# A fused FFT and two-layer kernel on one Trainium2 core: the beginning rearranged, with the first stage's stores ahead of the second weight chunk

## The chip, the cores and the metric

The kernel runs on 1 core of one Trainium2 chip (trn2). The metric is the time of one execution in device microseconds; below, "us" is microseconds. The core has a matrix engine (TensorE, PE in the profile, with its weight loads as PEld), a vector engine (VectorE, DVE), an activation engine (ScalarE, ACT), a general engine (GpSimd, POOL), and a queue engine (SyncE, SP) that issues most of the DMA transfers.

## The reference, cut to what matters

```
X = np.fft.fft(x, axis=1)            # x: (2, 3008, 256)
X = np.fft.fft(X, axis=2)
x = X.real.astype(np.float32).reshape(6016, 256)
h = x @ w_in                         # (256, 2048)
g = np.where(h > 0, h, np.exp(np.minimum(h, 0)) - 1)
x = g @ w_out                        # (2048, 256)
h = x @ w2_in
g = np.maximum(h, 0) + alpha * np.minimum(h, 0)
return g @ w2_out
```

The weights arrive as 64-bit floats, x as 32-bit floats.

## The kernel before

**The transform.** 3008 is 47 times 64, so the transform along the sequence is done in two stages. Stage A (`stage_a`) multiplies a chunk `xc` of x by the 47-point matrix `f47` on TensorE; ScalarE copies the result to `uc`; `store_u` writes it to memory (`ud`) with two axes exchanged, and `load_v` reads it back as `vt`, transposed. Batch 0 has four such chunks c = 0 to 3, each done in two halves i = 0, 1. Stage B (`stage_b`) multiplies `vt` by the 64-point matrix `r64`, in two halves q = 0, 1; ScalarE and VectorE split each result into a high and a low part (`zt`). The 256-point transform along the other axis isn't done on the data: it is multiplied into the first weights (`w_fold`: `c256` times a chunk of `w_in` gives `wi`, also as a high and a low part). `w_fold` also sends a row by memory to `an_sb`, which VectorE needs in the ticks. `delta_0` and `spread_0` make a correction row `zb`.

**The weights.** `w_in` and `w_out` are loaded (`ld`) in four chunks of 1 MB each. Before a chunk can be used, its 64-bit numbers are made 32-bit ones, half a chunk at a time: `conv_y` is one ScalarE instruction (L308), `conv_s` three VectorE ones (L325, L327, L329); `conv_h` does all four. For `w_out`, `w_split` then makes the high part on ScalarE (L380) and the low one on GpSimd (L381).

**The ticks.** Layer 1 is 96 ticks, one for each pair of a block of columns and a tile f of 128 hidden units. Tick t does, on TensorE, `gemm1` (L422, two banks of three multiplications) and at its end `gemm2` (L438, twelve) of tick t-3 (tick 0's stands at the end of tick 2). VectorE makes from the two banks `pt` (L555) and two tiles `ht` (L556, L557); ScalarE makes the exponential (L574, L576); VectorE combines (`combine`, L527), ScalarE splits off the high part (L534), GpSimd the low part (`lo`, L540). Tick 5 begins with stage B of the second block, and a small ScalarE copy `dt` (L218) of its correction. The second layer follows in 48 pairs.

**What sets the order.** Each engine works through its own list in the order in which the code is written. The list `START` is the order of the beginning; the tables `CONV1`, `FOLD` and others hang further steps into ticks, at their beginning (`pre`), middle (`mid`) or end (`end`). Fold c = 0 serves hidden tiles 0 to 3, fold 1 tiles 4 to 7 (first used in tick 4). PSUM has two banks `mmt` and two banks `eet` for everything but `gemm2`; `mmtile` hands them out in turn.

SyncE issues a transfer only when its wait has ended, and what stands behind it in the list waits too. Before the change the four stores of stage A of batch 0 are issued by ScalarE.

Of the kernel before, what the change touches and what calls it, by code (L numbers as in the profile page):

```python
# [28 lines left out]


START = [
# [3 lines left out]
    ('conv', 'i', 1, 0), ('conv', 'i', 1, 1), ('fold', 0), ('an', 0), ('fold', 1), ('delta',),  # L35
    ('conv', 'o', 0, 0),
    ('alpha',), ('u', 1), ('load', 'o', 1, 1), ('b',), ('conv', 'o', 0, 1), ('split', 'o', 0, 0), ('v', 1, 0, 32), ('load', 'x', 1, 0), ('u', 2),
    ('load', 'i', 1, 2), ('load', 'x', 1, 1), ('load', 'o', 1, 2), ('load', 'x', 1, 2), ('load', 'i', 1, 3), ('load', 'o', 1, 3),
    ('an', 1),
]  # L40


# [3 lines left out]


CONV1 = [
    (('o', 1, 0), None, (None, None, 1)),
    (('o', 1, 1), (3, 3, 5), (4, 4, 6)),  # L50
    (('i', 1, 2), (8, 8), (9, 9)),
    (('o', 1, 2), (13, 13, 15), (14, 14, 15)),
# [5 lines left out]
    (0, (7, 'pre'), (8, 'pre')), (1, (9, 'pre'), (11, 'pre')), (2, (12, 'pre'), (14, 'pre')), (3, (16, 'pre'), (17, 'pre')),  # L58
]
LOAD_X = {3: 9}  # L60
FOLD = {2: (11, 'pre', 0), 3: (18, 'pre', 0)}
LOAD_V = {(0, 2): 12, (1, 0): 24, (1, 1): 24, (1, 2): 24}
STAGE_B = {(0, 1): 5, (0, 2): 22, (1, 2): 32, (1, 0): 36, (1, 1): 40}
LOAD_ZB = {1: 6, 2: 29, 3: 45, 4: 61, 5: 77}
# [37 lines left out]
def tile_fft_moe_elu_moe_prelu(  # L102
# [72 lines left out]
    uc = {}  # L175

    def stage_a(b, c, i):

        if i == 0:
            uc[b, c] = big.tile([96, 8, 256], F32, tag="big", name="uc")  # L180
        for r0 in (4 * i, 4 * i + 2):
            p = mmtile()
            mm(out=p[0:96], lhsT=f47_sb, rhs=xc[b, c][0:96, r0:r0 + 2, :].rearrange("p r j -> p (r j)"),
               start=True, stop=True)
            act(out=uc[b, c][:, r0:r0 + 2, :].rearrange("p r j -> p (r j)"), in_=p[0:96], func=ACTF.Copy)
        if i == 1 and b == 1:
            for g in range(3):
                store_u(b, c, g)
        if i == 1 and b == 0:
            store_u(b, c, 0, nc.scalar)  # L190

    def store_u(b, c, g, eng=nc.sync):
        eng.dma_start(out=ud[b][g][c * 8:(c + 1) * 8].rearrange("n m j -> m n j"),
                      in_=uc[b, c][g * 32:(g + 1) * 32])


    vt = {}
# [58 lines left out]
    def stage_b(b, g):  # L256
        v = vt.pop((b, g))
        bl = BL[b, g]
        z = big.tile([128, 2, 2, 512], F32R, tag="big", name="zt")
        for q in range(2):  # L260
            p = mmtile()
            for k in range(4 * q, 4 * q + 4):
                o = p.rearrange("p (e k n) -> p e k n", e=2, k=4)[:, :, k % 4, :]
                mm(out=o, lhsT=v[:, k, 0:128], rhs=r64_sb[:, 0:128], start=True, stop=False)
                mm(out=o, lhsT=v[:, k, 128:256], rhs=r64_sb[:, 128:256], start=False, stop=True)
            pv = p.rearrange("p (e m) -> p e m", e=2)
            own = BLOCKS[bl][2] - (MOVED if bl == LONG else 0)
# [12 lines left out]
        zt[bl] = z  # L280
# [4 lines left out]

    def ld(kind, layer, c, eng):

        home, tag = (big, "big") if (kind, layer, c) in wd else (wp, f"w{kind}{c}")
        if kind == "i":
            src = (w_in, w2_in)[layer - 1][:, c * 512:(c + 1) * 512].bitcast(I32).rearrange("(k p) f -> p k f", p=128)  # L290
            t = home.tile([128, 2, 1024], I32, tag=tag, name="w64")
        else:
            src = (w_out, w2_out)[layer - 1][c * 512:(c + 1) * 512, :].bitcast(I32).rearrange("(k p) d -> p k d", p=128)
            t = home.tile([128, 4, 512], I32, tag=tag, name="w64")
        eng.dma_start(out=t, in_=src)
        raw[kind, layer, c] = t
        w32[kind, layer, c] = None
# [38 lines left out]
    def w_fold(c):  # L336

        t = w32.pop(("i", 1, c)).rearrange("p (k f) -> p k f", k=2)
        w = wp.tile([128, 2, 2, 512], F32R, tag=f"wi{c}", name=f"wi{c}")
        for e in (1, 0):  # L340
            p = mmtile()
            for k in range(2):
                mm(out=p, lhsT=c256_sb[:, k, e * 128:(e + 1) * 128], rhs=t[:, k, :], start=(k == 0), stop=(k == 1))
            if e == 1:
                at_ = wk.tile([1, 512], F32, tag="s", name="at", bufs=4)
                act(out=at_, in_=p[0:1, :], func=ACTF.Copy)
                nc.scalar.dma_start(out=ad[:, c * 512:(c + 1) * 512], in_=at_)
# [195 lines left out]
    def tick(t, pre, mid, end):  # L543
# [3 lines left out]
        if cur:  # L547
# [171 lines left out]
    with tc.manual_schedule():  # L719
# [192 lines left out]
```

## Time and profile before

| | |
|---|---|
| median of 3 runs | 976.53 us (976.29 to 977.09) |
| profiled execution, its own time | 976.22 us |
| its span | 974.3 us |
| TensorE busy | 952.8 us, 98% of the span |
| VectorE busy | 724.2 us, 74% |
| ScalarE busy | 653.4 us, 67% |
| GpSimd busy | 623.7 us, 64% |

The span runs from the first to the last instruction that the profile shows; the execution's own time is 1.9 us longer. A busy share is a mean over the whole span; the beginning, with which the change deals, is a small part of it and looks different.

### The profile page before, as it was taken

Reading aid. Unit: us, or ns where it says so; the run is one execution under the profiler, and the core shown is the slowest. Engines: PE = TensorE matmul, PEld = TensorE weight load, DVE = VectorE, ACT = ScalarE, POOL = GpSimd, SP = SyncE. Lnnn points to the kernel's source line nnn. Section 1 sums busy time; section 2 is a strip of 40 time slices with the busy share of each in tenths; the row PEclk is TensorE's granted clock in tenths of the full one; section 3 lists DMA queues with packets and bytes.
Section 4 is the critical chain, followed back from the end, with each engine's and each line's share of the span. In section 5 each row is a group of like instructions: output and inputs, shape, how many; then the busy total and the mean of one; then the engine's idle time right before and its main releaser. Section 6 shows DMA issues by size and latency. Waiting matters only on the chain.

```text
span 974.3 us, 12247 instructions
## 1 busy us (share of the span) xinstructions
PE 952.8 (98%) x4206; PEld 768.2 (79%) x4206; DVE 724.2 (74%) x1045; ACT 653.4 (67%) x925; POOL 623.7 (64%) x497
## 2 busy tenths in 40 slices
PE   9899999999999999999999999999999999999998
PEld 3576767789888877788878878889988887887886
DVE  2797989989999999887767766566756656566564
ACT  5577776676788878898766655555566565565553
POOL 1365667765777869887788755656656574664543
PEclk9999999999999999999999999999999999999999
DMA  8963322202212411121140020020010002001001
GB/s 322 332 207 83 90 77 87 98 1 87 60 58 80 167 44 33 44 86 44 44 152 1 1 81 1 1 87 1 1 45 38 1 1 87 1 2 43 1 1 44
DMA packets 27014, 64.11 MB, mean 66 GB/s; under 512 B 3076, under 2 KB 11524, under 8 KB 24776
## 3 DMA queue, kind: packets, MB, share of 16 engines
q1 hardware_dynamic: 25536, 62.09, 19.0%
q10 hardware_dynamic: 1160, 1.07, 0.4%
q8 instruction: 33, 0.54, 0.2%
q0 software_dynamic: 256, 0.17, 0.1%
q14 instruction: 29, 0.24, 0.1%
HBM read 41.53 MB, written 21.79 MB: 65 GB/s over the span
## 4 chain that ended last, share of the span: by engine, by line
PE 76%; DVE 14%; issue 4%; ACT 3%; DMA 3%; SPq 0%; POOL 0%; DVEq 0%; ACTq 0%
PE acc L438 43%; PE eet L611 13%; PE mmt L611 9%; PE mmt L422 7%; DVE ht L557 2%; DVE et L524 2%; DVE pt L555 2%; PE eet L422 2%; DVE et L527 1%; DMA w<-w_in 1%; DVE w L329 1%; DVE sg L327 1%; DVE sg L325 1%; DMA w<-w_out 1%; ACT hi L629 1%
## 5 line engine op out<-in xcount | busy, mean ns | idle before, releaser
L438 PE MATMUL acc<-hi,wo 128*128 128x512 f32 (+1 forms) x1536 | 469.5, 387 | 5.4 <-ACT hi L534 2.4
L635 POOL TENSOR_TENSOR lo<-et,hi 128x512 fp32r<-128x512 f32 (+1 forms) x190 | 237.2, 1280 | 187.0 <-ACT hi L629 187.0
L438 PEld LDWEIGHTS acc<-hi,wo 128*128 128x128 f32 x1536 | 288.7, 188 | 61.8 <-ACT hi L534 2.8
L540 POOL TENSOR_TENSOR lo<-et,hi 128x512 fp32r<-128x512 f32 (+1 forms) x192 | 267.3, 1415 | 102.5 <-ACT hi L534 50.4
L438 PE MATMUL acc<-lo,wo 128*128 128x512 f32 (+1 forms) x768 | 297.6, 388 | 2.8 <-POOL lo L540 2.6
L629 ACT ACTIVATE hi<-et 128x1024 fp32r<-128x1024 f32 (+1 forms) x96 | 99.5, 1043 | 115.9 <-PE acc L438 60.3
L438 PEld LDWEIGHTS acc<-lo,wo 128*128 128x128 f32 x768 | 144.8, 189 | 33.9 <-POOL lo L540 6.2
L574 ACT ACTIVATE et<-ht 128x1024 f32<-128x1024 f32 (+2 forms) x97 | 100.3, 1034 | 81.9 <-DVE ht L557 76.3
L656 DVE TENSOR_TENSOR v<-mmt,p 128x512 f32<-128x512 f32 (+1 forms) x48 | 32.7, 682 | 144.1 <-ACT p L652 143.9
L422 PE MATMUL mmt<-zt,wi 128*128 128x512 f32 (+1 forms) x462 | 122.8, 397 | 2.9 <-DVE ht L557 1.0
L422 PEld LDWEIGHTS mmt<-zt,wi 128*128 128x128 f32 x462 | 85.7, 188 | 27.0 <-DVE ht L557 4.4
L534 ACT ACTIVATE hi<-et 128x1024 fp32r<-128x1024 f32 (+2 forms) x97 | 99.2, 1023 | 3.9 <-DVE et L527 2.6
L677 ACT ACTIVATE et<-mmt 128x512 f32<-128x512 f32 (+1 forms) x96 | 55.9, 589 | 31.2 <-PE mmt L611 16.3
L527 DVE SCALAR_TENSOR_TENSOR et<-et,ht 128x1024 f32<-128x1024 f32 (+2 forms) x44 | 69.2, 1574 | 1.8 <-POOL lo L540 1.1
L555 DVE SCALAR_TENSOR_TENSOR pt<-zb,an_sb,mmt 128x512 f32<-128x512 f32 (+1 forms) x77 | 56.3, 732 | 14.9 <-PE mmt L422 14.6
L524 DVE SCALAR_TENSOR_TENSOR et<-eet,ht 128x512 f32<-128x512 f32 (+1 forms) x106 | 67.2, 676 | 0.0
L680 DVE SCALAR_TENSOR_TENSOR et<-et,oma_sb,eet 128x512 f32<-128x512 f32 (+1 forms) x96 | 66.3, 732 | 0.0
L680 DVE SCALAR_TENSOR_TENSOR et<-et,oma_sb,mmt 128x512 f32<-128x512 f32 (+1 forms) x96 | 66.1, 730 | 0.0
L581 ACT ACTIVATE eet<-et 128x512 f32<-128x512 f32 (+1 forms) x106 | 58.9, 588 | 3.7 <-DVE et L524 2.1
L611 PE MATMUL mmt<-xo,wi 128*128 128x512 f32 (+1 forms) x216 | 60.2, 387 | 1.0 <-ACT p L652 1.0
L611 PE MATMUL eet<-xo,wi 128*128 128x512 f32 (+1 forms) x216 | 60.2, 387 | 0.0
L611 PE MATMUL eet<-xo,sx 128*128 128x512 f32 (+1 forms) x216 | 59.7, 385 | 0.0
(120 smaller groups left out, 1287.5 us busy)
## 6 DMA issues: line engine op xcount, KB each, us to landing
w<-w_in SPq DMA_DIRECT2D x8, 1024.0 KB, 5.9
w<-w_out SPq DMA_DIRECT2D x8, 1024.0 KB, 7.7
vt<-ud SPq DMA_DIRECT2D x6, 1024.0 KB, 4.8
ud<-uc SPq DMA_DIRECT2D x20, 256.0 KB, 4.2
xd<-xs SPq DMA_DIRECT2D x10, 512.0 KB, 3.1
xs<-xd SPq DMA_DIRECT2D x5, 1024.0 KB, 8.4
out_t<-ot SPq DMA_DIRECT2D x16, 256.0 KB, 2.2
xc<-x SPq DMA_DIRECT2D x5, 768.0 KB, 7.9
```

Of the source, the lines that this page charges most:

```text
L422: mm(out=p[:, 0:n], lhsT=lhsT, rhs=rhs, start=(i == 0), stop=(i == len(ops) - 1))
L438: mm(out=accs[L, bl][d][t][:, 0:n], lhsT=w[:, a, o, d * 128:(d + 1) * 128], rhs=(hi, lo)[b][:, t, 0:n], start=(f == first and i == 0), sto ...
L524: stt(out=s["e"][:, i, :], in0=s["x"][i], scalar=-1.0, in1=s["h"][:, i, :], op0=ALU.add, op1=ALU.max)
L527: stt(out=s["e"][:, i], in0=s["e"][:, i], scalar=-1.0, in1=s["h"][:, i], op0=ALU.add, op1=ALU.max)
L534: act(out=s["hi"][:, i, 0:s["n"]], in_=s["e"][:, i], func=ACTF.Copy)
L540: nc.gpsimd.tensor_tensor(out=s["lo"][:, i, 0:n], in0=s["e"][:, i, :], in1=s["hi"][:, i, 0:n].bitcast(F32), op=ALU.subtract)
L555: stt(out=pt[:, 0:n], in0=zb[bl][:, 0:n], scalar=an_sb[:, f:f + 1], in1=p[0], op0=ALU.mult, op1=ALU.add)
L574: act(out=s["e"][:, i], in_=s["h"][:, i], func=ACTF.Relu, scale=-1.0)
L611: mm(out=bank[:, 0:n], lhsT=w[:, a], rhs=x2[b][:, 0:n], start=(first and m == 0), stop=(last and m == 2), skip_group_check=True)
L629: act(out=s["hi"][f][:, :, 0:n], in_=s["g"][f], func=ACTF.Copy)
L635: eng.tensor_tensor(out=s["lo"][f][:, t, 0:n], in0=s["g"][f][:, t], in1=s["hi"][f][:, t, 0:n].bitcast(F32), op=ALU.subtract)
L680: stt(out=o, in0=o, scalar=oma_sb[:, 2 * j + f:2 * j + f + 1], in1=h, op0=ALU.mult, op1=ALU.add)
```

## The change

It rewrites the order of the beginning.

- The four stores of stage A of batch 0 go from ScalarE's queue to SyncE's, where they stand ahead of the load of the second chunk of `w_in` (before, that load was issued at the start). The store of the last chunk is cut in two, one for each half i.
- The transposed read `vt` is cut in two: its rows 0 to 24 of 32, which depend on the first three chunks, and rows 24 to 32.
- Fold 1 leaves the beginning and goes to the start of tick 1, behind `combine(0)`; the conversion of its chunk stands in and behind stage B (one half between its two halves, one half after it).
- The conversion and split of the first `w_out` chunk leave the beginning: half 0 goes to tick 0, half 1 to ticks 2 and 3. The raw chunk is loaded into another buffer (`wo3`).
- `w_fold` works on both banks by turns (first half of the weights for both, then the second half).
- `combine(0)` and the split of tick 0 move from behind tick 1's `pt` and `ht` to the start of tick 1.

```diff
 START = [
-    ('r64',), ('eye',), ('load', 'i', 1, 0), ('c256',), ('load', 'i', 1, 1),
-    ('a', 0, 0), ('a', 0, 1), ('a', 1, 0), ('a', 1, 1), ('a', 2, 0), ('a', 2, 1), ('conv', 'i', 0, 0), ('conv', 'i', 0, 1), ('a', 3, 0),
-    ('a', 3, 1), ('v', 0, 0, 32), ('load', 'o', 1, 0),
-    ('conv', 'i', 1, 0), ('conv', 'i', 1, 1), ('fold', 0), ('an', 0), ('fold', 1), ('delta',),
-    ('conv', 'o', 0, 0),
-    ('alpha',), ('u', 1), ('load', 'o', 1, 1), ('b',), ('conv', 'o', 0, 1), ('split', 'o', 0, 0), ('v', 1, 0, 32), ('load', 'x', 1, 0), ('u', 2),
+    ('r64',), ('eye',), ('load', 'i', 1, 0), ('c256',),
+    ('a', 0, 0), ('a', 0, 1), ('a', 1, 0), ('a', 1, 1), ('a', 2, 0), ('a', 2, 1),
+    ('conv', 'i', 0, 0), ('conv', 'i', 0, 1), ('a', 3, 0), ('a', 3, 1), ('v', 0, 0, 24), ('v', 0, 24, 32),
+    ('load', 'i', 1, 1), ('load', 'o', 1, 0), ('alpha',), ('u', 1), ('load', 'o', 1, 1),
+    ('fold', 0), ('an', 0), ('delta',), ('b',), ('conv', 'i', 1, 1),
+    ('v', 1, 0, 32), ('load', 'x', 1, 0), ('u', 2),
...
 CONV1 = [
-    (('o', 1, 0), None, (None, None, 1)),
+    (('o', 1, 0), (0, 0, 0), (2, 2, 3)),
...
-FOLD = {2: (11, 'pre', 0), 3: (18, 'pre', 0)}
+FOLD = {1: (1, 'pre', 1), 2: (11, 'pre', 0), 3: (18, 'pre', 0)}
...
-        if i == 1 and b == 0:
-            store_u(b, c, 0, nc.scalar)
+        if b == 0 and c == 3:
+            store_u(b, c, 0, rows=(4 * i, 4 * i + 4))
+        elif b == 0 and i == 1:
+            store_u(b, c, 0)
...
             if q == 0 and b == g == 0:
                 spread_0()
+                conv_h("i", 1, 1, 0)
...
-        home, tag = (big, "big") if (kind, layer, c) in wd else (wp, f"w{kind}{c}")
+        home, tag = (big, "big") if (kind, layer, c) in wd else (wp, "wo3" if (kind, layer, c) == ("o", 1, 0) else f"w{kind}{c}")
...
+        banks = {1: mmtile(), 0: mmtile()}
+        for k in range(2):
+            for e in (1, 0):
+                mm(out=banks[e], lhsT=c256_sb[:, k, e * 128:(e + 1) * 128], rhs=t[:, k, :], start=(k == 0), stop=(k == 1))
...
-        if t == 1:
-            combine(0)
-            split_hi(0)
-            split_lo(0)
...
+        at(1, combine, 0)
         for c, (t, where, n) in FOLD.items():
             at(t, w_fold, c, where=where)
             at(t + n, load_an, c, nc.gpsimd, where='end')
+        at(1, split_hi, 0)
+        at(1, split_lo, 0)
```

On SyncE, behind the first loads of x, the list before reads as follows (`w` is a raw weight chunk, `c_sb` the 256-point matrix, `al_sb` a vector that is used much later).

```order
L295 DMA w_129<-w_in 128x2x1024
L745 DMA c_sb<-c 128x2x256
L295 DMA w_132<-w_in 128x2x1024
L203 DMA vt<-ud_81 128x2048
L295 DMA w_203<-w_out 128x4x512
L742 DMA al_sb<-alpha 128x16
L193 DMA ud_82<-uc 32x8x256 x4
L295 DMA w_262<-w_out 128x4x512
```

And now:

```order
L298 DMA w_129<-w_in 128x2x1024
L746 DMA c_sb<-c 128x2x256
L195 DMA ud_81<-uc 32x8x256 x3
L195 DMA ud_81<-uc 32x4x256 x2
L205 DMA vt<-ud_81 96x2048
L205 DMA vt<-ud_81 32x2048
L298 DMA w_203<-w_in 128x2x1024
L298 DMA w_205<-w_out 128x4x512
L743 DMA al_sb<-alpha 128x16
L195 DMA ud_82<-uc 32x8x256 x4
L298 DMA w_212<-w_out 128x4x512
```

The second `w_in` chunk has moved from ahead of the read of `vt` to behind both its parts, and the stores of stage A stand ahead of that read.

On TensorE, from the end of stage A to the correction row (L232), the list before holds two folds (eight multiplications of `c_sb`).

```order
L183 MATMUL mmt<-xc,f_sb 96x512
L343 MATMUL mmt<-w_176,c_sb 128x512 x2
L343 MATMUL eet<-w_176,c_sb 128x512 x2
L343 MATMUL eet<-w_205,c_sb 128x512 x2
L343 MATMUL mmt<-w_205,c_sb 128x512 x2
L232 MATMUL mmt<-r_sb,vt 8x64
```

Now it holds one fold there, and the other stands behind the two banks of tick 0's `gemm1` (L427).

```order
L182 MATMUL mmt<-xc,f_sb 96x512
L346 MATMUL mmt<-w_174,c_sb 128x512
L346 MATMUL eet<-w_174,c_sb 128x512
L346 MATMUL mmt<-w_174,c_sb 128x512
L346 MATMUL eet<-w_174,c_sb 128x512
L234 MATMUL eet<-r_sb,vt 8x64
...
L427 MATMUL eet<-zt,wi_214 128x512 x3
L427 MATMUL mmt<-zt,wi_214 128x512 x3
L346 MATMUL mmt<-w_250,c_sb 128x512
L346 MATMUL eet<-w_250,c_sb 128x512
L346 MATMUL mmt<-w_250,c_sb 128x512
L346 MATMUL eet<-w_250,c_sb 128x512
```

Four multiplications of `c_sb` have left the place between stage A and the correction row.

On VectorE, from tick 0's `pt` to tick 2's, the list before is this.

```order
L555 SCALAR_TENSOR_TENSOR pt<-zb,an_sb,mmt 128x512
L556 TENSOR_TENSOR ht<-pt,eet 128x512
L557 TENSOR_TENSOR ht<-pt,eet 128x512
L555 SCALAR_TENSOR_TENSOR pt<-zb,an_sb,eet 128x512
L556 TENSOR_TENSOR ht<-pt,mmt 128x512
L557 TENSOR_TENSOR ht<-pt,mmt 128x512
L527 SCALAR_TENSOR_TENSOR et<-et,ht 128x512 x2
L555 SCALAR_TENSOR_TENSOR pt<-zb,an_sb,mmt 128x512
```

And now (`w_205` is the first chunk of `w_out`, `wi_321` the result of fold 1):

```order
L560 SCALAR_TENSOR_TENSOR pt<-zb,an_sb,eet 128x512
L561 TENSOR_TENSOR ht<-pt,mmt 128x512
L562 TENSOR_TENSOR ht<-pt,mmt 128x512
L328 TENSOR_SCALAR sg<-w_205 128x512
L330 SCALAR_TENSOR_TENSOR sg<-w_205,sg 128x512
L332 SCALAR_TENSOR_TENSOR w_306<-w_306,sg 128x512
L532 SCALAR_TENSOR_TENSOR et<-et,ht 128x512 x2
L354 TENSOR_TENSOR wi_321<-mmt,wi_321 128x512
L354 TENSOR_TENSOR wi_321<-eet,wi_321 128x512
L560 SCALAR_TENSOR_TENSOR pt<-zb,an_sb,eet 128x512
L561 TENSOR_TENSOR ht<-pt,mmt 128x512
```

Between tick 0's `ht` and tick 1's `pt` three steps of a conversion and two of the fold have come in, and `combine(0)` (`et`) stands ahead of tick 1's `pt`. Half 1 of the same conversion, three more, now stands between tick 2's `combine(1)` and tick 3's `pt`.

## Rows read from the trace of the kernel before

**Rows 1.** The page's first line: the span.
```profile
span 974.3 us, 12247 instructions
```
**Rows 2.** Stretches of the span: length, then each engine's busy time, clock, DMA.
```profile
50.00:60.00 10.00, 8.38 (x53) 6.40 (x52) 9.62 (x12) 5.84 (x7) 5.28 (x4) 1.00 0.85 227
60.00:70.00 10.00, 10.00 (x42) 7.49 (x41) 8.71 (x12) 7.63 (x9) 5.72 (x4) 1.00 0.67 238
```
**Rows 3.** TensorE in time: start, length, instruction, idle before and its releaser.
```profile
42.59 3.16 PE L438 MATMUL acc<-hi,wo 128*128 128x512 f32 x8 [2.37 <-ACT hi L534]
59.65 0.96 PE L422 MATMUL eet<-zt,wi 128*128 128x512 f32 x3 [0.98 <-ACT dt L218]
```
**Rows 4.** TensorE and the queues in time, end of stage A to stage B.
```profile
19.84 0.59 ACT L185 ACTIVATE uc<-mmt 96x512 f32<-96x512 f32 x1
...
22.08 2.74 PE L343 MATMUL eet<-w,c_sb 128*128 128x512 f32 x6
...
23.27 0.34 SPq L203 DMA_DIRECT2D vt<-ud  x1
...
28.16 0.27 PE L232 MATMUL mmt<-r_sb,vt 128*8 128x64 f32 x2 [0.35 <-DMA vt<-ud]
...
30.46 1.12 PE L239 MATMUL eet<-eye 8*128 8x512 f32 x2
...
33.17 0.39 PE L265 MATMUL mmt<-r_sb,vt 128*128 128x128 f32 x2
```
**Rows 5.** DMA issues of short stretches: KB each, us from issue to landing.
```profile
f_sb<-f SPq DMA_DIRECT2D x1, 36.0 KB, 1.7
...
xc<-x SPq DMA_DIRECT2D x1, 256.0 KB, 2.9
...
ud<-uc ACTq DMA_DIRECT2D x1, 256.0 KB, 7.7
...
ud<-uc ACTq DMA_DIRECT2D x1, 256.0 KB, 2.7
...
an_sb<-ad POOLq DMA_DIRECT2D x1, 2.0 KB, 6.1
```
**Rows 6.** VectorE in time, from fold 0 to the first tick.
```profile
24.84 0.69 DVE L349 TENSOR_TENSOR wi<-mmt,wi 128x512 fp32r<-128x512 f32 x1
25.44 0.68 DVE L349 TENSOR_TENSOR wi<-eet,wi 128x512 fp32r<-128x512 f32 x1
...
32.13 0.43 DVE L325 TENSOR_SCALAR sg<-w 128x512 int32<-128x512 int32 x1 [2.37 <-DMA w<-w_out]
...
34.00 0.69 DVE L275 TENSOR_TENSOR zt<-eet,zt 128x512 fp32r<-128x512 f32 x1
...
37.06 0.74 DVE L555 SCALAR_TENSOR_TENSOR pt<-zb,an_sb,mmt 128x512 f32<-128x512 f32 x1
```
**Rows 7.** VectorE in time, ticks 1 to 4.
```profile
45.21 1.23 DVE L527 SCALAR_TENSOR_TENSOR et<-et,ht 128x1024 f32<-128x1024 f32 x1 [0.69 <-ACT et L576]
...
47.92 0.75 DVE L555 SCALAR_TENSOR_TENSOR pt<-zb,an_sb,eet 128x512 f32<-128x512 f32 x1 [1.49 <-PE eet L422]
...
51.11 1.51 DVE L325 TENSOR_SCALAR sg<-w 128x512 int32<-128x512 int32 x1
...
55.13 0.74 DVE L555 SCALAR_TENSOR_TENSOR pt<-zb,an_sb,mmt 128x512 f32<-128x512 f32 x1
```
**Rows 8.** ScalarE in time: fold 1 before.
```profile
26.14 0.59 ACT L346 ACTIVATE at<-eet 1x512 f32<-1x512 f32 x1 [1.54 <-PE eet L343]
...
27.04 0.60 ACT L348 ACTIVATE wi<-eet 128x512 fp32r<-128x512 f32 x1 [0.31 <-ACT at L346]
```
**Rows 9.** GpSimd in time: two pairs of `lo`.
```profile
42.63 2.53 POOL L540 TENSOR_TENSOR lo<-et,hi 128x512 fp32r<-128x512 f32 x2 [3.44 <-ACT hi L534]
...
48.76 3.57 POOL L540 TENSOR_TENSOR lo<-et,hi 128x512 fp32r<-128x512 f32 x2 [1.18 <-ACT hi L534]
```
**Rows 10.** A stretch after the longest idle time of TensorE (columns of rows 2).
```profile
43.30:46.70 3.40, 3.40 (x10) 2.65 (x9) 2.45 (x3) 3.34 (x5) 2.78 (x3) 0.51 1.08 367
```

More of the change, by code (lines that the diff above doesn't have):

```diff
@@ L31 @@
 START = [
[3 rows of a table removed]
-    ('conv', 'i', 1, 0), ('conv', 'i', 1, 1), ('fold', 0), ('an', 0), ('fold', 1), ('delta',),
-    ('conv', 'o', 0, 0),
-    ('alpha',), ('u', 1), ('load', 'o', 1, 1), ('b',), ('conv', 'o', 0, 1), ('split', 'o', 0, 0), ('v', 1, 0, 32), ('load', 'x', 1, 0), ('u', 2),
[6 rows of a table added]
     ('load', 'i', 1, 2), ('load', 'x', 1, 1), ('load', 'o', 1, 2), ('load', 'x', 1, 2), ('load', 'i', 1, 3), ('load', 'o', 1, 3),
-    ('an', 1),
 ]
@@ L188, in stage_a, with store_u @@
                 store_u(b, c, g)
-        if i == 1 and b == 0:
-            store_u(b, c, 0, nc.scalar)
-    def store_u(b, c, g, eng=nc.sync):
-        eng.dma_start(out=ud[b][g][c * 8:(c + 1) * 8].rearrange("n m j -> m n j"),
-                      in_=uc[b, c][g * 32:(g + 1) * 32])
+        if b == 0 and c == 3:
+            store_u(b, c, 0, rows=(4 * i, 4 * i + 4))
+        elif b == 0 and i == 1:
+            store_u(b, c, 0)
+    def store_u(b, c, g, rows=(0, 8)):
+        r0, r1 = rows
+        nc.sync.dma_start(out=ud[b][g][c * 8 + r0:c * 8 + r1].rearrange("n m j -> m n j"),
+                          in_=uc[b, c][g * 32:(g + 1) * 32, r0:r1])
     vt = {}
@@ L339, in w_fold @@
         w = wp.tile([128, 2, 2, 512], F32R, tag=f"wi{c}", name=f"wi{c}")
+        banks = {1: mmtile(), 0: mmtile()}
+        for k in range(2):
+            for e in (1, 0):
+                mm(out=banks[e], lhsT=c256_sb[:, k, e * 128:(e + 1) * 128], rhs=t[:, k, :], start=(k == 0), stop=(k == 1))
         for e in (1, 0):
-            p = mmtile()
-            for k in range(2):
-                mm(out=p, lhsT=c256_sb[:, k, e * 128:(e + 1) * 128], rhs=t[:, k, :], start=(k == 0), stop=(k == 1))
+            p = banks[e]
             if e == 1:
```

## The prediction

> **What bounds the kernel now.** I read the page first, then the stretches of the span, and then the beginning engine by engine in order of time. The span is 974.3 us [rows 1]. From 60 to 70 us TensorE is busy 10.00 of 10 us, from 50 to 60 only 8.38, while VectorE has 9.62 there [rows 2]. So there is a point near 60 us behind which TensorE sets the time, and ahead of which something else does. The last wait before it is the one of the matmul at 59.65 (tick 5's second bank), 0.98 us for ScalarE's `dt` [rows 3]. Behind it the lists of all engines are the same before and after. So the change is worth what it moves this matmul, one for one, and all that follows is about where it goes. The span's own execution took 976.22 us, 0.31 less than the median of the runs; I add the shift to both.
>
> Ahead of that point I follow VectorE by two marks: tick 0's `pt` at 37.06 [rows 6] and tick 4's at 55.13 [rows 7]. From tick 4's `pt` to the matmul at 59.65 (two `ht`, the exponential, `dt`) nothing is edited. From mark to mark it is 18.07 us, in which VectorE waits twice: 0.69 for ScalarE and 1.49 for TensorE [rows 7].
>
> What puts mark one at 37.06? The correction row starts when `vt` has landed, at 28.16, and stage B's first half is done at 30.46 [rows 4]. But its low part comes only at 34.00, since the conversion of the first `w_out` chunk stands ahead of it and that chunk lands at 32.13 [rows 6]. So the beginning waits first for the transposed read, then for a weight chunk that isn't needed yet.
>
> **The read comes sooner.** Stage A ends as now, at 19.84 + 0.59 = 20.43 [rows 4]: its x is loaded ahead of all that moves. Today's last store holds 256 KB and lands in 2.7 us [rows 5]; the read is issued at 23.27, which is 0.14 later [rows 4]. The new last store holds 128 KB. 36 KB took 1.7 [rows 5], so 128 KB lies between 1.7 and 2.7; I take 2.1, on a straight line. The second part of the read is then issued at 20.43 + 2.1 + 0.14 = 22.7. It holds 256 KB, and a load of that size took 2.9 [rows 5]: 25.6. The first part, 768 KB, is issued near 20.9 and has 4.7 us; the whole 1 MB takes 28.16 - 23.27 = 4.9 [rows 4], so it is no later. Correction row at 25.6 (bounds 25.2 to 26.2), 2.5 us sooner.
>
> The other stores cost nothing, though they now stand in one queue behind `w_in` and `c256`: one that was issued beside the loads took 7.7 us already [rows 5], and only the last is waited for. ScalarE's four issues go away in ScalarE's idle time of a stage that TensorE paces.
>
> **From there to tick 0's `pt`.** Stage B's first half takes 30.46 - 28.16 = 2.3 us: 27.9. ScalarE's copy adds 0.6, and VectorE makes the first low part at 28.5. Such an instruction occupies VectorE for 0.60 (24.84 to 25.44), and the three steps of half a conversion for 34.00 - 32.13 = 1.87 [rows 6]. So: first steps of the second `w_in` chunk 29.1 to 31.0; the second half of stage B ends 33.56 - 30.46 = 3.1 us behind the first [rows 4], at 31.0, its copy at 31.6; second low part to 32.2; three more steps to 34.1. Mark one goes from 37.06 to 34.1: **-3.0** (bounds -3.4 and -2.4).
>
> This holds if three transfers come in time. The second `w_in` chunk is issued right behind the read. A chunk in that place (`w_out`) now lands 32.13 - 28.16 = 4.0 us behind the read, which would be 29.6 against 29.1; the 0.6 us for which VectorE waits for stage B covers that. `w_out` follows by at most 4.0, at 33.6, and ScalarE wants it ahead of tick 0's exponential, near 35.5. `an_sb` took 6.1 us from its issue [rows 5], which now comes near 25.5: 31.6, against 34.1. Were one of these covers gone, each microsecond of lateness would count in full, because VectorE and ScalarE work in order.
>
> **Inside the ticks.** Five things change between the marks.
>
> The conversion of the first `w_out` chunk comes in: two halves, 2 x 1.87 = 3.74. Fold 1's two low parts come in: 2 x 0.60 = 1.20. Together **+4.9**. Until now this work stood ahead of mark one, mostly in time in which VectorE waited for `vt` and `w_out` anyway.
>
> The 1.49 us wait for TensorE goes: three conversion steps (1.87) now stand ahead of that very `pt`. The 0.69 wait shrinks to about 0.3: tick 1's exponential takes some 2.2 us after its `ht`, and tick 2's `pt` and two `ht` fill 2.0. Together **-1.9** (bounds -2.2 and -0.7).
>
> A new wait: fold 1's low parts follow ScalarE's high parts. On ScalarE, behind the last conversion step, stand the split of `w_out` (0.5), `at` with its issue (27.04 - 26.14 = 0.90) and a copy of 0.6 [rows 8]: some 2.1 us, while VectorE has two `combine` of 0.6 to do. **+1.0** (bounds 0 and 1.4). Behind it on VectorE stands tick 1's `pt`, and all later ticks wait.
>
> Fold 1's four matmuls, 2.74 / 3 = 0.9 us each [rows 4], go in between two ticks of TensorE. They cost nothing there: TensorE is ahead of VectorE and waits for the banks that VectorE frees. Uncovered they would cost 3.6. That `combine(0)` moves ahead makes ScalarE's and GpSimd's split of tick 0 sooner, but TensorE can use it only behind tick 2's `gemm1`, so it gives nothing. The order within the fold, likewise, moves less than a microsecond on an engine that then waits for the read.
>
> VectorE and GpSimd disturb each other: a step L325 took 1.51 us instead of 0.43 [rows 6, 7], and the pair of `lo` beside it 3.57 instead of 2.53 [rows 9]. The moved steps of half 0 come ahead of the first `lo`, those of half 1 behind tick 0's pair, so I charge 0; the upper bound is two such meetings, +2.2. [...]
>
> **Sum**: -3.0 + 4.9 - 1.9 + 1.0 = +1.0, with the roundings +1.1. The matmul at 59.65 comes near 60.7. The profiled execution would take 977.3 us, the median of the runs 977.6; I predict 977.4, which is 0.1% slower. A measurement of this kernel can tell about 0.2%, or 2 us, from no change: so no change, from what is gained ahead of the ticks and lost in them. For the forecast alone: 976.7 to 978.4.
>
> **Rivals.**
>
> *TensorE's clock falls ahead of stage B (slower).* Fold 0 ends near 19.7 + 3.6 = 23.3, and with fold 1 gone nothing stands between it and the read at 25.6: 2.3 us of idle time. Now the wait there is 0.35 [rows 4]. [...] It decides if the read lands at 25.6 or later; a read at 24.5 would leave half the idle time. [...] Chance 0.25. [...]
>
> *VectorE isn't what binds in the ticks (faster).* Then the 4.9 us hide in waits that I don't see, and the 3.0 ahead of mark one reach the end: 973.5. Against it: 9.62 of 10 us busy [rows 2], and only 2.2 us of waits between the marks. Chance 0.10.
>
> *The read isn't sooner.* If the stores in SyncE's queue wait for the loads ahead of them longer than I think, or two parts cost more than one, `vt` lands at 28.1 as now, and only the loss remains: 1.1 + 2.5, 980.1. Chance 0.05.
>
> *The waits absorb more.* Without the new wait, and with a read at 25.2, the sum lies between -0.6 and +0.2: 976.0 to 976.7. Chance 0.10.
>
> **How the numbers follow.** The forecast has 0.50. Slower by over 0.2% (above 978.5): most of the first rival, the third, and the forecast's edge by meetings with GpSimd, 0.31. Faster by over 0.2% (below 974.6): most of the second, 0.09. Within: 0.60. For 8 in 10 I leave out the second and third rivals and the top of the first: 975.2 to 979.6.
>
> **What would show it.** Right: the correction row starts near 25.6 and tick 0's `pt` near 34; `pt` of tick 4 near 56; VectorE in one piece from 34 to 56, with a wait of about 1 us for ScalarE ahead of fold 1's low parts; the matmul behind `dt` near 60.7. [...] Wrong would be `vt` far from 25.6, a wait of VectorE for `w_in` or `an_sb`, or a tick 4 `pt` at 53 or sooner.

## The result, and the profile after

The changed kernel takes 982.03 us, the median of 6 runs (981.44 to 984.53), against 976.41 for the kernel before: a ratio of 1.0065 (95% interval 1.0051 to 1.0079). It is 5.6 us slower, where 977.4 was predicted and 979.6 was the upper end of the range.

The page's first line, the span:

```profile
span 980.5 us, 12256 instructions
```

TensorE in time, from the last fold to the point behind which it sets the time (start, length, instruction; in brackets the idle time before it and what ended it):

```profile
22.35 1.02 PE L346 MATMUL eet<-w,c_sb 128*128 128x512 f32 x2
28.69 0.37 PE L234 MATMUL eet<-r_sb,vt 128*8 128x64 f32 x2 [5.32 <-DMA vt<-ud]
...
32.92 1.52 PE L241 MATMUL mmt<-eye 8*128 8x512 f32 x2
...
65.60 0.96 PE L427 MATMUL eet<-zt,wi 128*128 128x512 f32 x3 [0.98 <-ACT dt L220]
```

The last row answers to the matmul at 59.65 in [rows 3], and waits for the same `dt` as long as it did: a shift of +5.95. The span grew by 980.5 - 974.3 = 6.2, so nearly all of the loss lies ahead of this point, as the prediction assumed. Within it, the correction row starts at 28.69; 28.16 was its time before [rows 4], 25.6 the forecast. TensorE idles 5.32 us ahead of it.

VectorE in time, the two marks and what lies between them:

```profile
39.55 0.74 DVE L560 SCALAR_TENSOR_TENSOR pt<-zb,an_sb,eet 128x512 f32<-128x512 f32 x1
...
45.60 0.69 DVE L354 TENSOR_TENSOR wi<-mmt,wi 128x512 fp32r<-128x512 f32 x1 [0.86 <-ACT wi L353]
...
51.18 1.23 DVE L532 SCALAR_TENSOR_TENSOR et<-et,ht 128x1024 f32<-128x1024 f32 x1 [0.16 <-ACT et L577]
...
56.23 2.16 DVE L532 SCALAR_TENSOR_TENSOR et<-et,ht 128x1024 f32<-128x1024 f32 x1
...
59.57 1.59 DVE L332 SCALAR_TENSOR_TENSOR w<-w,sg 128x512 int32<-128x512 int32 x1
61.08 0.73 DVE L560 SCALAR_TENSOR_TENSOR pt<-zb,an_sb,mmt 128x512 f32<-128x512 f32 x1
```

Tick 0's `pt` stands at 39.55: 2.49 later than the 37.06 of [rows 6], where the forecast had 3.0 sooner. From mark to mark it is 61.08 - 39.55 = 21.53, against 18.07 before, or +3.46; the forecast was +4.0. So the ticks went as reckoned, and the 5.5 us of error lie ahead of tick 0.

The chain that ended last, from stage A's last store on, shows where they begin:

```profile
20.59 1.95 DMA ud<-uc
...
22.59 5.96 DMA vt<-ud
...
28.69 0.37 PE eet L234 x2
```

The store took 1.95 (forecast 2.1) and the second part of the read was issued at 22.59 (forecast 22.7). But from issue to landing it took 5.96 us, where I had put 2.9. Two stretches of the span, one in the read and one in stage B:

```profile
24.00:27.00 3.00, 0.00 (x0) 0.00 (x0) 1.29 (x2) 0.77 (x2) 0.94 (x1) 0.99 0.94 208
...
26.90:33.70 6.80, 5.01 (x21) 4.32 (x22) 0.73 (x2) 0.60 (x1) 0.78 (x1) 0.50 1.03 359
```

The DMA engines are busy 0.94 of the first stretch and move only 208 GB/s. In the second the granted clock is 0.50 through all of stage B's first half. So two questions: why is the read slow, and what does the low clock cost?

### The profile page after: what moved, and what is told of

Its sections match the earlier page's. It is cut to its first block, busy times and chain, and to the rows that moved or that the text cites. A ratio compares the mean times of both kernels' runs of the same rounds, so it can differ in the third digit from the quotient of the medians.

```text
span 980.5 us, 12256 instructions
## 1 busy us (share of the span) xinstructions
PE 954.7 (97%) x4206; PEld 770.0 (79%) x4206; DVE 724.8 (74%) x1045; ACT 652.8 (67%) x925; POOL 623.0 (64%) x497
## 4 chain that ended last, share of the span: by engine, by line
PE 77%; DVE 12%; ACT 4%; issue 3%; DMA 2%; SPq 0%; POOL 0%; DVEq 0%; ACTq 0%
PE acc L443 44%; PE eet L612 12%; PE mmt L612 9%; PE mmt L427 7%; DVE et L529 2%; DVE ht L562 2%; DVE pt L560 2%; PE eet L427 2%; DMA w<-w_in 1%; DVE w L332 1%; DVE sg L330 1%; ACT et L575 1%; PE eet L182 1%; DVE et L532 1%; ACT hi L630 1%
## 5 line engine op out<-in xcount | busy, mean ns | idle before, releaser
L427 PE MATMUL mmt<-zt,wi 128*128 128x512 f32 (+1 forms) x462 | 122.8, 397 | 4.4 <-DVE wi L354 2.5
L427 PEld LDWEIGHTS mmt<-zt,wi 128*128 128x128 f32 x462 | 85.5, 188 | 28.5 <-DVE ht L562 5.0
```

The lines of the kernel that those rows point to most:

```text
L427: mm(out=p[:, 0:n], lhsT=lhsT, rhs=rhs, start=(i == 0), stop=(i == len(ops) - 1))
```

## The experiments

The marks of every run, from the same rows as above (us; "row" is the correction row's first matmul, "last" the matmul behind `dt`), and the medians. Beside them on the same chip the kernel before took 977.02 (e1 to e4), 976.60 (e5 to e8) and 976.49 (e9, e10); the last column is the distance of each median from that (the changed kernel's from its 976.41). The marks are those of one execution, the profiled one.

| kernel | row | tick 0's pt | tick 4's pt | last | median | over before |
|---|---|---|---|---|---|---|
| before | 28.16 | 37.06 | 55.13 | 59.65 | 976.41 | 0 |
| changed | 28.69 | 39.55 | 61.08 | 65.60 | 982.03 | +5.62 |
| e2_fill | 28.38 | 36.91 | 58.46 | 62.98 | 979.82 | +2.80 |
| e1_one_read | 27.94 | 38.03 | 59.57 | 64.09 | 981.49 | +4.47 |
| e3_one_read_fill | 28.14 | 36.67 | 58.21 | 62.73 | 980.23 | +3.21 |
| e5_cols | 28.24 | 39.01 | 60.54 | 65.06 | 981.49 | +4.89 |
| e6_p64 | 28.67 | 41.50 | 63.05 | 67.57 | 984.97 (one run) | +8.37 |
| e4_conv_only | 28.33 | 35.68 | 54.69 | 59.22 | 977.61 | +0.59 |
| e8_combine | 28.36 | 35.71 | 55.12 | 59.65 | 977.26 | +0.66 |
| e9_fold_only | 28.39 | 37.03 | 59.04 | 63.57 | 982.01 | +5.52 |
| e10_repaired | 28.70 | 35.15 | 56.69 | 61.21 | 978.14 | +1.65 |
| e7_best | 30.51 | 34.92 | 54.33 | 58.85 | 976.10 | -0.50 |

In e7 and e10 the correction row stands behind stage B's first half.

### What the low clock costs: e2_fill

```diff
+    def fill(n):
+        p = pa.tile([128, 512], F32, tag="acc00", name="fill")
+        for i in range(n):
+            mm(out=p, lhsT=c256_sb[:, 0, 0:128], rhs=c256_sb.rearrange("p k f -> p (k f)"), start=(i == 0), stop=(i == n - 1))
...
-    ('fold', 0), ('an', 0), ('delta',), ('b',), ('conv', 'i', 1, 1),
+    ('fold', 0), ('an', 0), ('fill', 6), ('delta',), ('b',), ('conv', 'i', 1, 1),
```

> The changed kernel with six more multiplications of the 256-point matrix by itself on TensorE between fold 0 and the correction row (some 5.2 us of work into a bank that nobody reads), so that TensorE isn't idle while it waits for vt. Theory 1 (the idle time of 5.3 us makes the granted clock fall, and the low clock costs what stage B loses): granted clock 1.0 from 20 to 40 us, stage B's first half 2.3 us instead of 3.9 (from the correction row at 28.7 to the bank's last column), tick 0's pt near 37.7 instead of 39.55, time about 980.1. Theory 2 (the low clock costs nothing, because VectorE and ScalarE set the pace here): pt stays at 39.5, time 982.

TensorE in time and the stretch of stage B in e2_fill:

```profile
23.13 5.31 PE L723 MATMUL fill<-c_sb 128*128 128x512 f32 x12
28.38 0.28 PE L234 MATMUL eet<-r_sb,vt 128*8 128x64 f32 x2
...
30.68 1.12 PE L241 MATMUL mmt<-eye 8*128 8x512 f32 x2
```

```profile
26.90:33.70 6.80, 6.80 (x42) 4.61 (x40) 2.82 (x5) 1.76 (x3) 0.78 (x1) 1.00 1.05 361
```

Work that nobody needs makes the kernel 2.8 us faster (5.62 over the kernel before becomes 2.80). The granted clock stays at 1.00, stage B's first half takes 30.68 - 28.38 = 2.30 instead of 32.92 - 28.69 = 4.23, and from the correction row to tick 0's `pt` it is 8.53 instead of 10.86. Theory 1 holds. Of the 2.64 us by which `pt` is sooner, 2.33 are the clock and 0.31 an earlier correction row, which here follows the filling work without idle time.

### Why the read is slow: e1_one_read, e5_cols, e6_p64, e3_one_read_fill

One read again (e1), two parts cut along the row so that each covers all 128 partitions (e5), and the partitions cut 64 + 64 instead of 96 + 32 (e6). e3 is e1 with four of e2's multiplications.

```diff
-    ('conv', 'i', 0, 0), ('conv', 'i', 0, 1), ('a', 3, 0), ('a', 3, 1), ('v', 0, 0, 24), ('v', 0, 24, 32),
+    ('conv', 'i', 0, 0), ('conv', 'i', 0, 1), ('a', 3, 0), ('a', 3, 1), ('v', 0, 0, 32),
```

> The changed kernel with the read of vt in one part again (all 128 partitions, behind both halves of the last store). In the changed kernel the parts are issued at 21.08 and 22.59 and the last lands at 28.6, 6.0 us behind its issue. Theory 1 (the cut itself makes the transfer slow: 96 and then 32 partitions instead of 128): the one read is issued near 22.6 and takes the 4.8 us it took before the change, lands near 27.4, the correction row starts 1.2 us sooner than 28.69, and the time falls from 982.0 to about 980.8. Theory 2 (the read is slow because of what shares the DMA engines with it, the stores ahead and the second weight chunk behind, whatever its shape): it lands at 28.6 or later, time 982 or more. In both the clock still falls to half in stage B, since TensorE idles as long.

```diff
+    def load_v_cols(g, k0, k1):
...
+        nc.sync.dma_start(out=vt[0, g][:, k0:k1], in_=ud[0][g].rearrange("n (q k) j -> (n q) k j", k=8)[:, k0:k1])
...
-    ('conv', 'i', 0, 0), ('conv', 'i', 0, 1), ('a', 3, 0), ('a', 3, 1), ('v', 0, 0, 24), ('v', 0, 24, 32),
+    ('conv', 'i', 0, 0), ('conv', 'i', 0, 1), ('a', 3, 0), ('a', 3, 1), ('vc', 0, 0, 4), ('vc', 0, 4, 8),
```

> The changed kernel with the read of vt still in two parts, but cut along the row instead of across the partitions: both parts go to all 128 partitions and hold 512 KB each, and both wait for the last store. Theory 1 (parts that cover 96 and 32 of the 128 partitions move slowly; two parts as such cost nothing): the parts are issued from 22.7 and the last lands at 27.8 as the one read did, the correction row starts at 27.9 to 28.1, time 981.3, like the one read. Theory 2 (two transfers in place of one cost the extra time): it lands at 28.6 again, correction row 28.7, time 982.

```diff
-    ('conv', 'i', 0, 0), ('conv', 'i', 0, 1), ('a', 3, 0), ('a', 3, 1), ('v', 0, 0, 24), ('v', 0, 24, 32),
+    ('conv', 'i', 0, 0), ('conv', 'i', 0, 1), ('a', 3, 0), ('a', 3, 1), ('v', 0, 0, 16), ('v', 0, 16, 32),
```

> The changed kernel with the cut across the partitions moved from 96 + 32 to 64 + 64. Theory 1 (a part that covers only some of the partitions moves slowly): each of the two parts of 512 KB again takes well over the 4.9 us from issue to landing that the whole 1 MB took; the first is issued near 21.1 and lands after 26, the second lands near 28. Theory 2 (shape is no matter): the first part, issued 1.5 us ahead of the second, lands by 25, and the second by 27.5.

> Both together: one read, and four such multiplications (3.4 us, so that they end ahead of the read's landing). If the two causes are right and add, the correction row starts near 27.5, tick 0's pt stands near 36.5, and the time is about 979.0: the rest above the kernel before is then what the work moved into the ticks costs, with a beginning that is only 0.7 us sooner instead of the 3.0 forecast. If the rivals hold, 982.

The same stretch of each (24 to 27 us, GB/s at the end), where the changed kernel has 208. First e1, one read:

```profile
24.00:27.00 3.00, 0.00 (x0) 0.00 (x0) 1.29 (x2) 0.98 (x2) 0.94 (x1) 1.00 0.84 319
```

e5, cut along the row:

```profile
24.00:27.00 3.00, 0.00 (x0) 0.00 (x0) 1.29 (x2) 0.53 (x2) 1.72 (x2) 0.88 1.00 315
```

e6, 64 + 64 partitions:

```profile
24.00:27.00 3.00, 0.00 (x0) 0.00 (x0) 1.29 (x2) 0.86 (x2) 0.94 (x1) 1.00 1.02 218
```

Two transfers that cover all partitions move 315 GB/s, like one (319). Two that cover 64 partitions each move 218, with the DMA engines no less busy (1.02 of the stretch). So the cut across the partitions makes the read slow, and not the number of parts: theory 1. But its worth is small. The chain that ended last in e1 and in e6:

```profile
22.88 4.92 DMA vt<-ud
...
27.94 0.37 PE eet L234 x2
```

```profile
22.74 5.79 DMA vt<-ud
...
28.67 0.37 PE eet L234 x2
```

The whole megabyte takes 4.92 in e1, about what it took before the change (28.16 - 23.27 = 4.9). It is issued only 0.39 sooner than before, at 22.88, so `vt` is there 0.2 us sooner (27.94 against 28.16), and 0.75 ahead of the changed kernel. The time falls by 0.5, or by 1.15 over the kernel before (5.62 becomes 4.47); theory 1 had 1.2. By the marks the last matmul comes 1.51 sooner, 0.75 by the read and 0.77 by a low clock that costs less, but what lies behind it takes 0.7 longer, and the intervals of the two ratios overlap (1.0041 to 1.0067 against 1.0051 to 1.0079): the marks show this gain, the times don't. In e5 the correction row is at 28.24 and the last matmul 0.97 later than in e1, with the same median. e5 differs from the changed kernel in one thing more, as its first part is issued behind the last store, at 22.44 instead of 21.08. e3, with the clock kept up, has its row at 28.14 and takes 980.23: e2's gain, and no more for the one read than executions differ. Its 979.0 was a miss: the row came 0.6 later than expected but `pt` only 0.2, and behind its last matmul the span takes 1.1 longer than before (978.5 - 62.73 = 915.8 against 914.65).

Why a read that is cut across the partitions moves more slowly, and in what order its parts move, no run shows.

### The parts of the change in the ticks: e4_conv_only, e9_fold_only, e8_combine

e4 is the kernel before with the conversion of the first `w_out` chunk moved into the ticks; e9 the kernel before with fold 1 moved (and `combine(0)` ahead of it), and four multiplications that nobody reads in fold 1's old place.

```diff
-    ('conv', 'o', 0, 0),
-    ('alpha',), ('u', 1), ('load', 'o', 1, 1), ('b',), ('conv', 'o', 0, 1), ('split', 'o', 0, 0), ('v', 1, 0, 32), ('load', 'x', 1, 0), ('u', 2),
+    ('alpha',), ('u', 1), ('load', 'o', 1, 1), ('b',), ('v', 1, 0, 32), ('load', 'x', 1, 0), ('u', 2),
...
-    (('o', 1, 0), None, (None, None, 1)),
+    (('o', 1, 0), (0, 0, 0), (2, 2, 3)),
```

> The kernel before with one part of the change: the conversion and split of the first w_out chunk go from the beginning to ticks 0, 2 and 3 (fold 1, the stores and the read stay as before). By the prediction's sums: stage B no longer waits for w_out, tick 0's pt comes at about 35.3 instead of 37.06 (-1.7); 3.74 us of VectorE work come into the ticks (+3.7), the waits of 1.49 and 0.69 go (-1.9): +0.1, time 976.5, the same. Rival: the work in the ticks costs its full length, as VectorE's waits come back elsewhere: +2, 978.4. Other rival: the moved work hides in waits wholly, -1.7: 974.7.

```diff
-    ('conv', 'i', 1, 0), ('conv', 'i', 1, 1), ('fold', 0), ('an', 0), ('fold', 1), ('delta',),
+    ('conv', 'i', 1, 0), ('conv', 'i', 1, 1), ('fold', 0), ('an', 0), ('fill', 4), ('delta',),
...
-    ('an', 1),
...
-FOLD = {2: (11, 'pre', 0), 3: (18, 'pre', 0)}
+FOLD = {1: (1, 'pre', 1), 2: (11, 'pre', 0), 3: (18, 'pre', 0)}
```

> The kernel before with the other part of the change alone: fold 1 goes from the beginning to the start of tick 1, behind combine(0) (whose split moves ahead with it), and four multiplications that nobody reads stand in its place on TensorE, so that TensorE is as busy there as before. Stores, read, and the conversion of w_out stay as they were. Tick 0's pt stays at 37. From it to tick 4's pt: by the prediction's sums 1.2 us of low parts and a wait of 1.0 for ScalarE come in (+2.2) and the waits of 0.69 and 1.49 (2.2) absorb some of it, 18.07 becomes 18.5 to 20.3, time 977 to 979. Rival, from the kernel with everything moved: there the stretch was 21.53, and 19.01 with the conversion alone, so the fold cost 2.5 beyond it; then 18.07 becomes 20.6 or more and the time is 979 to 980: the waits that the prediction let absorb the fold don't absorb it.

The conversion alone, VectorE's marks in e4:

```profile
35.68 0.75 DVE L554 SCALAR_TENSOR_TENSOR pt<-zb,an_sb,mmt 128x512 f32<-128x512 f32 x1 [0.59 <-PE mmt L421]
...
54.69 0.74 DVE L554 SCALAR_TENSOR_TENSOR pt<-zb,an_sb,mmt 128x512 f32<-128x512 f32 x1
```

Tick 0's `pt` stands at 35.68 (-1.4, forecast 35.3), mark to mark 19.01 (+0.94, forecast +1.8), and the time 977.61 against 977.02, a ratio of 1.0009 (1.0000 to 1.0018): no change, as its first theory had it. (Its last matmul stands 0.43 sooner than before, but its span is 975.4, 1.1 longer.) Fold 1 alone: `pt` stays at 37.03, and mark to mark is 22.01, +3.94. VectorE in e9, where the ticks begin and at tick 4:

```profile
39.92 0.69 DVE L526 SCALAR_TENSOR_TENSOR et<-et,ht 128x512 f32<-128x512 f32 x1 [0.76 <-ACT et L571]
41.11 0.69 DVE L526 SCALAR_TENSOR_TENSOR et<-et,ht 128x512 f32<-128x512 f32 x1 [0.49 <-ACT et L571]
43.89 0.69 DVE L348 TENSOR_TENSOR wi<-mmt,wi 128x512 fp32r<-128x512 f32 x1 [2.08 <-ACT wi L347]
...
59.04 0.75 DVE L554 SCALAR_TENSOR_TENSOR pt<-zb,an_sb,mmt 128x512 f32<-128x512 f32 x1 [0.35 <-DMA an_sb<-ad]
```

The fold opens waits for ScalarE of 0.76 + 0.49 + 2.08 = 3.3 us, and at the end one of 0.35 for `an_sb`. In the changed kernel one of 0.86 is left at this place; there the conversion's three steps stand ahead of `combine(0)`, where e9 has the first of these waits. So the two parts don't add: 0.94 alone and 3.94 alone make 3.46 together. The fold is the dear one: 22.01 lies in the rival's "20.6 or more", and the time beyond both theories. The shift of the last matmul (63.57 - 59.65 = 3.9) fits the profiled execution, which took 980.26 and is the fastest of the five; why the others took longer (median 982.01, up to 984.48) is open. By that median the fold alone would lose as much as the whole change.

e8 is e4 with `combine(0)` and the split of tick 0 ahead of tick 1's `pt`:

```diff
-        if t == 1:
-            combine(0)
-            split_hi(0)
-            split_lo(0)
...
+        at(1, combine, 0)
+        at(1, split_hi, 0)
+        at(1, split_lo, 0)
```

> The kernel with only the conversion moved (e4_conv_only), and combine(0) with the split of tick 0 ahead of tick 1's pt, as the change has it. In e4_conv_only TensorE waited 4.01 us for tick 0's high part at 43.07, and the granted clock was 0.5 from 41.9 to 48.7. By the prediction combine(0) gives nothing by moving. Rival: the high part comes 2.5 us sooner, the idle time and the low clock shrink, VectorE's wait of 0.66 for tick 3's bank goes, and the time falls from 977.6 to 976.5 or less.

TensorE's first multiplication with tick 0's high part, in e4 and then in e8:

```profile
43.07 3.78 PE L437 MATMUL acc<-hi,wo 128*128 128x512 f32 x8 [4.01 <-ACT hi L533]
```

```profile
41.03 0.50 PE L437 MATMUL acc<-hi,wo 128*128 128x512 f32 x1 [1.93 <-ACT hi L533]
```

Its wait falls from 4.01 us to 1.93, but VectorE's marks don't gain (tick 4's `pt` at 55.12 against 54.69). The time is 977.26, against 977.61 without it, and both lie 0.6 to 0.7 above the kernel before beside them: no gain, as the prediction said of this step.

Two parts of the change have no run of their own: the stores' other queue together with the later load of the second `w_in` chunk, and the order within `w_fold`, which e9 has as before.

### The beginning mended: e10_repaired, and a version of the kernel before: e7_best

e10 has the changed kernel's ticks, the read cut along the row, stage B's first half ahead of the correction row, and four of e2's multiplications. e7 has e8's ticks and the same read and order of stage B, with stores and fold 1 as before.

```diff
-    ('conv', 'i', 0, 0), ('conv', 'i', 0, 1), ('a', 3, 0), ('a', 3, 1), ('v', 0, 0, 24), ('v', 0, 24, 32),
+    ('conv', 'i', 0, 0), ('conv', 'i', 0, 1), ('a', 3, 0), ('a', 3, 1), ('vc', 0, 0, 4), ('vc', 0, 4, 8),
...
-    ('fold', 0), ('an', 0), ('delta',), ('b',), ('conv', 'i', 1, 1),
+    ('fold', 0), ('an', 0), ('fill', 4), ('b',), ('conv', 'i', 1, 1),
...
             if q == 0 and b == g == 0:
-                spread_0()
+                delta_0(v)
                 conv_h("i", 1, 1, 0)
+        if b == g == 0:
+            spread_0()
```

> The changed kernel with its beginning mended by what the runs show: the read of vt cut along the row (two parts of 512 KB, all partitions), stage B's first half ahead of the correction row, and four multiplications that nobody reads on TensorE until the first part is there. The ticks are the changed kernel's. The first part lands near 26.6, stage B starts near 26.8 at a granted clock of 1.0, and tick 0's pt comes behind the second w_in chunk (30.9) and its two half conversions: near 35.5 instead of 39.55, and tick 4's pt 21.5 later, near 57. Time near 978.3, still 1.5 us above the kernel before, because the ticks cost 3.5 more and the beginning gives back less than 2. If the beginning were what makes the change lose, it would now be equal to the kernel before or faster: 976.5 or less.

> A version made from what the runs show: e8_combine (stores and fold 1 as before the change, the conversion of the first w_out chunk in the ticks, combine(0) early), with the read of vt cut along the row into two parts of 512 KB, and stage B's first half, which needs only the first part, ahead of the correction row; the spread of that row comes behind the second half. TensorE finishes fold 1 at 27.7, so stage B can start there instead of at 28.6, and its second half doesn't wait for the row's way over VectorE (1.1 us): tick 0's pt near 34.0 instead of 35.68 in e4_conv_only, and the time 1.5 to 2 us below e8_combine's, near 975. If something else binds there (an_sb, which lands at 32.7, or w_out), pt stays above 35 and the time is e8_combine's.

VectorE in e10, the two marks:

```profile
35.15 0.74 DVE L566 SCALAR_TENSOR_TENSOR pt<-zb,an_sb,eet 128x512 f32<-128x512 f32 x1
...
56.69 0.73 DVE L566 SCALAR_TENSOR_TENSOR pt<-zb,an_sb,mmt 128x512 f32<-128x512 f32 x1
```

The mended beginning brings tick 0's `pt` to 35.15, 1.9 us sooner than before the change, and the ticks take 21.54, as in the changed kernel (21.53). The time is 978.14, a ratio of 1.0017 (1.0008 to 1.0026): 4.0 of the 5.6 us are back, and what stays is the ticks' 3.47 less the 1.9.

e7 brings tick 4's `pt` to 54.33 and the last matmul to 58.85, 0.8 sooner than before, but its span is 975.0, 0.7 longer. Its median is 976.10 against 976.60, a ratio of 0.9998 (0.9989 to 1.0007): no measurable gain, 975 was a miss. The profiled execution is the slowest of its eleven. In it VectorE is still 0.6 us ahead of the kernel before at 288 us and 0.7 behind at 293. Most of that is one conversion step, first in the kernel before, then in e7:

```profile
292.02 0.44 DVE L325 TENSOR_SCALAR sg<-w 128x512 int32<-128x512 int32 x1
```

```profile
291.79 1.35 DVE L330 TENSOR_SCALAR sg<-w 128x512 int32<-128x512 int32 x1
```

e3 has the same 1.35 at this step. TensorE's lead over the kernel before falls behind it from 0.6 us to nothing (307.36 against 307.30), though it shows no idle time there. So VectorE can still count behind 60 us; why the step is slow in one kernel and not in the other wasn't tested.

## Why the prediction was wrong, point by point

**What bounds: right.** From tick 4's `pt` to the matmul behind `dt` it is 65.60 - 61.08 = 4.52, and was 59.65 - 55.13 = 4.52; behind it the span changed by 0.25 (914.9 against 914.65). In the experiments the rest moved by up to 1.5 us (e4, e7), so "one for one" holds only to about that.

**The read comes sooner: the step that failed.** "It holds 256 KB, and a load of that size took 2.9: 25.6." The issue was right to 0.1 us, the transfer took 5.96. The step priced a part by its bytes alone. It left out that the first part was still on the same engines, and that parts on 96 and 32 partitions move slower than one on 128 (208 against 319 GB/s). That the first part was still moving, the packets of the changed kernel from 24 to 27 us show:

```profile
DMA packets 112, 0.62 MB, mean 208 GB/s; under 512 B 25, under 2 KB 25, under 8 KB 47
```

A row of `vt` is 8 KB (2048 numbers), and what else moves there comes in pieces of at most 4 KB. So 112 - 47 = 65 packets are rows of `vt` (65 of 8 KB and 47 - 25 = 22 of 4 KB make up the 0.62 MB): 520 KB behind 24 us, twice the second part. The bound of 26.2 was worked out by the same rule, so it didn't hold either. No shape tried came near 25.6 with the whole of `vt`: 27.94 to 28.24 with all partitions. Of the 2.5 us forecast at this place 0.2 was to be had, and the cut made it a loss of 0.5. This is 3.1 us of the 5.5; 0.75 of it is the cut (28.69 - 27.94), and the other 2.3 is that a read of the whole, issued behind the last store, took 4.9 in e1 (5.3 in e3).

**The clock: a rival that came in, at a higher price.** The rival gave a low clock ahead of stage B 0.25. It happened in each of the four kernels that left TensorE idle there (for 5.32 us in the changed kernel, 4.36 in e1, 5.10 in e5, 5.22 in e6; the second pair of stage B's matmuls took 0.63 us in all four) and in none with the filling work (0.39 us in e2, e3, e9 and e10), though e3 still had 1.33 us of idle time. By [rows 10] the price would be 1.7 (3.4 us at 0.51 do the work of 1.7), and the upper end of the range counts with that; no run shows it. In the changed kernel it was 2.33, since the low clock lasted 6.8 us, 5.01 of them with work, and not 3.4. It differs from kernel to kernel: from the row to `pt` e1 takes 10.09, or 1.56 more than with the clock kept up, and e6 12.83, or 4.30 more. That is most of why e6, whose row is the changed kernel's, is the slowest. Its low clock:

```profile
27.66:37.90 10.24, 9.23 (x36) 7.33 (x37) 3.09 (x5) 1.74 (x3) 0.78 (x1) 0.50 1.01 346
```

Its condition, a read at 25.6 or later, was the likeliest case by the forecast's own number, and the late read of the first point made the idle time more than twice as long. Whether the forecast's 2.3 us alone would have brought it, the runs leave open (last section). The two causes met, and the rivals had been counted one at a time.

**From the row to tick 0's `pt`: right, but by luck.** Forecast 34.1 - 25.6 = 8.5; with the clock kept up 8.53 (e2) and 36.67 - 28.14 = 8.53 (e3). The sum also wanted the second `w_in` chunk at 29.6. It came later, and only the late row hid that. In e10 stage B starts at 26.75, and ScalarE waits for the chunk (VectorE's first step starts at 30.82 too):

```profile
30.82 0.67 ACT L317 ACTIVATE w<-w 128x512 f32<-128x512 f32 x1 [1.41 <-DMA w<-w_in]
```

In the changed kernel, too, the chunk took 7.9 us from its issue at 22.95. So behind a row at 25.6 the conversion would have started 1.7 us later than the 29.1 of the sum, and `pt` would hardly have come before e10's 35.15 (an estimate from these rows): a gain of 1.9, not 3.0.

**Inside the ticks: right in sum, +3.46 against +4.0.** The new wait for ScalarE was 0.86 (forecast 1.0); the 1.49 went, the 0.69 became 0.16 (together -2.0, forecast -1.9). Meetings with GpSimd cost 2.16 - 1.22 and 1.59 - 0.69, 1.8 us, about the two of before (1.51 - 0.43 and 1.75 - 0.69, 2.1): no change, as charged. (In the changed kernel a pair of `lo` runs on GpSimd from 54.79, the split of `w_out` from 59.16.) The steps before that these sums use, beside those of [rows 7]:

```profile
49.98 1.22 DVE L527 SCALAR_TENSOR_TENSOR et<-et,ht 128x1024 f32<-128x1024 f32 x1
...
52.66 0.69 DVE L327 SCALAR_TENSOR_TENSOR sg<-w,sg 128x512 int32<-128x512 int32 x1
53.46 1.75 DVE L329 SCALAR_TENSOR_TENSOR w<-w,sg 128x512 int32<-128x512 int32 x1
```

So moving the conversion into the ticks didn't add to these meetings (1.8 us against 2.1). What the sum didn't show is that the parts can't be counted alone: e9 and e4 give 3.94 and 0.94.

**The sum.** -3.0 became +2.5, of which the read makes 3.1 and the clock 2.4 of the difference; the ticks were 0.5 better. 1.1 + 3.1 + 2.4 - 0.5 = 6.1, against the 6.2 of the span. The range was too narrow because the two rivals on the slow side were taken as alternatives: with 1.7 for the low clock (by [rows 10]) and the third rival's 2.5 both together give 977.4 + 1.7 + 2.5 = 981.6, near the 982.0 measured, though both prices were too low and the ticks 0.5 better.

## What to carry to other kernels

Price a transfer by the partitions that it covers as well as by its bytes: a load cut across the partitions so that its first part can start early may land later than the whole (here the row at 28.69 against 27.94). When work is taken out of a wait, TensorE, left idle, may come back at half its clock (here 0.50 behind 5.32 us without work), so ask what the next work on it is, and whether that is on the path; here useless multiplications gave 2.8 us back. And where two bad cases have the same trigger (here a late read), their prices add, and the range must reach to the sum.

## What the runs showed of the hardware

That TensorE stayed at the low clock while it was fully busy was new to me. In the changed kernel:

```profile
28.70:32.90 4.20, 4.20 (x20) 3.78 (x20) 0.68 (x1) 0.00 (x0) 0.47 (x1) 0.50 1.04 381
```

It works through all of 4.20 us, on stage B's small matmuls, and is granted 0.50 to the end. In e6 it works without idle time for 9.23 us, from 28.67 to 37.90, and is granted 0.50 throughout. In the kernel before, the stretch of [rows 10] behind the longest idle time was only 3.4 us long.

Nor did an idle time of one length always bring the low clock. In e3 and in e10 TensorE waits at the same place of the ticks for fold 1's low part, 2.51 us and 2.49 us. The wait and the stretch behind it, first of e3, then of e10:

```profile
43.47 0.96 PE L427 MATMUL mmt<-zt,wi 128*128 128x512 f32 x3 [2.51 <-DVE wi L354]
...
43.40:46.80 3.40, 3.33 (x14) 2.74 (x15) 3.21 (x6) 1.50 (x3) 3.32 (x3) 1.00 0.82 251
```

```profile
41.95 1.22 PE L433 MATMUL mmt<-zt,wi 128*128 128x512 f32 x3 [2.49 <-DVE wi L360]
...
42.47:45.88 3.41, 3.41 (x9) 2.64 (x9) 3.17 (x6) 1.48 (x3) 3.29 (x4) 0.50 0.96 284
```

The one keeps 1.00, the other falls to 0.50. There it costs nothing that shows: from mark to mark both take 21.54, and VectorE sets the pace (busy for 19.65 of them in e10, TensorE for 18.35). In e9 even a longer wait at that place, 3.31 us, is followed by 1.00:

```profile
44.63 0.96 PE L421 MATMUL mmt<-zt,wi 128*128 128x512 f32 x3 [3.31 <-DVE wi L348]
...
44.63:48.04 3.41, 3.41 (x15) 2.85 (x16) 3.17 (x6) 0.76 (x1) 0.95 (x1) 1.00 0.69 211
```
